# Output weights of three heads gathered onto chosen partitions in a cached attention block

## The chip, the cores and the metric

The kernel runs on one core of one Trainium2 chip. The metric is the device time of one execution in microseconds: 1310.93 us before the change, the median of 3 runs (1310.82 to 1311.02). All data is float32. The core's engines are TensorE (PE, matmuls), VectorE (DVE), ScalarE (ACT), GpSimd (POOL) and SyncE (SP, which issues nearly all transfers here), and it has 16 DMA engines that move data between HBM and the on-chip memory of 128 partitions.

## The reference

One token for each of two batch rows goes through a layer norm, then through attention over a cache of 32,768 keys and values, and through a gated projection:

```python
B, Sq, D = 2, 1, 512
Hq, Hkv, Sk, Dh = 32, 8, 32768, 128
xn = _layernorm(x)
q = (xn @ wq).reshape(B, Sq, Hq, Dh).transpose(0, 2, 1, 3)
scores = einsum("bhqd,bhkd->bhqk", q, k) * Dh ** -0.5      # 4 query heads share one key head
o = einsum("bhqk,bhkd->bhqd", softmax(scores), v)
s = o.transpose(0, 2, 1, 3).reshape(B, Sq, Hq * Dh) @ wo   # wo: 4096 x 512
h = relu(xn @ w1 + b1) ** 2                                # w1: 512 x 1792
g = silu(h @ w2 + b2)
out = x + s * g
```

The keys and the values are 268 MB each. `wo`, the output weights, is 8.4 MB: 32 heads of 128 rows of 512 numbers.

## The kernel before

The work goes in 16 steps `s`, one for each pair of key head and batch row (`hkv, b = divmod(s, B)`). For a step the keys come as two transfers of 8 MB (`load_k`, 64 KB for each of the 128 partitions, into three half slots `kslots`) and the values as two of 8 MB (`load_v`, into the one buffer `vbuf`). The main loop runs over 64 quarters `n` of keys: VectorE transposes the keys (L278), TensorE multiplies them with the queries (L283). After four quarters `softmax(s)` and `probs(s)` make the probabilities, and `values(m)` multiplies a values chunk with them (L358), two chunks behind. The queries stand in one of two buffers `qz`, which GpSimd fills for each step (`set_q`, L261).

All transfers of weights and cache stand in one list, `loads`, in the order in which SP issues them. An entry goes out when the event it names has passed in the program; the buffer's last reader is waited for on the chip. The last entries are the values of the last step and the output weights, which take the place of the keys.

The output projection is spread over 128 partitions. For eight heads at a time `load_wo(i)` gives each partition eight consecutive rows of `wo` (`"(p j) e -> p j e"`), and the attention output is laid out to match (`spread`, into `oW`). Head 0 stands apart: the rows of `wo` for the heads 1 to 31 go through `load_wo`, in pieces of 8, 8, 8 and then 4, 2 and 1 heads (`PIECES`, L138 and L142), while the 128 rows of head 0 come in the middle of the run. Ahead of the values chunks 8, 14, 20 and 26 (`FEW`) `load_few` issues two small transfers of 8 rows of 4 KB (two rows of `wo` together), onto the partitions 0 to 7 and 32 to 39 of the tile `few` (L148). `values` multiplies them (the matmuls of `project`, L403, into `few_ps`), multiplies by the gate and adds to the result `xe` (L347, L348). The selection of head 0's outputs for these partitions is `oF`, made in the branch `hkv == 0` of `values` (L384).

At the end the 24 + 7 heads of the wide loads are multiplied into `a_ps` (L403), multiplied by the gate (L468), added (L469) and stored (L471).

Of the kernel before, what the change touches and what calls it, by code (L numbers as in the profile page):

```python
# [8 lines left out]

F32 = mybir.dt.float32  # L10
AF = mybir.ActivationFunctionType
ALU = mybir.AluOpType
AX = mybir.AxisListType

P = 128
# [17 lines left out]

PIECES = ((0, 4), (4, 2), (6, 1))
FEW = (8, 14, 20, 26)
LAST = ((0, 64), (64, 128))

# [2 lines left out]
def gqa_decode_kernel(ctx: ExitStack, tc: tile.TileContext, x, kc, vc, wq, wo, w1, b1, w2, b2, out):  # L42
    nc = tc.nc
    B, _, D = x.shape
    _, HKV, SK, DH = kc.shape
    HQ = wq.shape[1] // DH
# [8 lines left out]
    WG = 8  # L55
    NWG = HQ // WG
# [6 lines left out]
    const = ctx.enter_context(tc.tile_pool(name="const", bufs=1))  # L63
    ktpool = ctx.enter_context(tc.tile_pool(name="ktpool", bufs=8))
    work = ctx.enter_context(tc.tile_pool(name="work", bufs=2))
# [66 lines left out]
    def load_wo(i):  # L132
        if i % 2 == 0:
            wide[i // 2] = kslots[:, 2 - i].rearrange("p (i j e) -> p i j e", i=2, j=WG)
        t = wide[i // 2][:, i % 2]
        base = (i * WG + 1) * P
        if i < NWG - 1:
            nc.sync.dma_start(t, wo[base:base + WG * P, :].rearrange("(p j) e -> p j e", p=P))  # L138
        else:
            for h0, nh in PIECES:  # L140
                lo = base + h0 * P
                nc.sync.dma_start(t[:, h0:h0 + nh, :], wo[lo:lo + nh * P, :].rearrange("(p j) e -> p j e", p=P))  # L142
        return t

    def load_few(i):
        for q in range(2):
            lo = 64 * q
            nc.sync.dma_start(few[32 * q:32 * q + 8].rearrange("p j e -> p (j e)"),  # L148
                              wo[lo:lo + 64, :].rearrange("(n y w j) e -> w y n (j e)", y=2, w=4, j=2)[i])

    wide = {}
    NK, NV = NS * NT, NS * NCH
    kslots = const.tile([P, 3, HALF], F32, name="kslots")
    few = const.tile([40, 2, D], F32, name="few")
    nc.gpsimd.memset(few, 0.0)
    vbuf = const.tile([P, 2 * HALF], F32, name="vbuf")
    loads = [(None, load_wq, 0), (None, load_half, 0), (None, load_half, 1), (("q", 0), load_w1, 0),
# [26 lines left out]
    ident = const.tile([P, P], F32, name="ident")  # L184
# [12 lines left out]
    selj = const.tile([P, WG], F32, name="selj")  # L197
    nc.vector.tensor_reduce(selj, ident.rearrange("p (e j) -> p j e", j=WG), axis=AX.X, op=ALU.add)
    sele = const.tile([P, P // WG], F32, name="sele")
    nc.vector.tensor_reduce(sele, ident.rearrange("p (e j) -> p e j", j=WG), axis=AX.X, op=ALU.add)  # L200
    sels = {}
    for nh in (4, 2):
        sels[nh] = const.tile([P, P // nh + nh], F32, name=f"sel_{nh}")
        nc.vector.tensor_reduce(sels[nh][:, 0:P // nh], ident.rearrange("p (e j) -> p e j", j=nh), axis=AX.X, op=ALU.add)
        nc.vector.tensor_reduce(sels[nh][:, P // nh:], ident.rearrange("p (e j) -> p j e", j=nh), axis=AX.X, op=ALU.add)
    oT = const.tile([P, HQ, B], F32, name="oT")
    oW = const.tile([P, NWG, WG, 16], F32, name="oW")
    nc.gpsimd.memset(oW, 0.0)
    oF = const.tile([40, WG, 32], F32, name="oF")
    nc.gpsimd.memset(oF, 0.0)  # L210
    sc = [pone.tile([P, 512], F32, tag=f"sc{i}", name=f"sc{i}") for i in range(NT)]
    o_ps = [pone.tile([P, 512], F32, tag=f"o{i}", name=f"o_ps{i}") for i in range(2)]
# [17 lines left out]
    t_ps = misc("xnT_ps")  # L230
# [107 lines left out]
    def values(n):  # L338
        s, k = divmod(n, NCH)
        vt = take(load_v, n)  # L340
        if n in FEW:
            i = FEW.index(n)
            take(load_few, i)
            t_ps = misc(f"few_ps{i}")
            project(t_ps, oF[:, 2 * i:2 * i + 2], few, 0, 2, start=True, stop=True)
            m = work.tile([P, DE], F32, tag="e", bufs=1, name=f"few{i}")
            nc.vector.tensor_mul(m, gate, t_ps[:, :DE])  # L347
            nc.vector.tensor_add(xe, m, xe)  # L348
        o = o_ps[s % 2]
# [12 lines left out]
        if k == NCH - 1:  # L362
            hkv, b = divmod(s, B)
            o_sb = work.tile([P, 512], F32, tag="o_sb", bufs=1, name=f"o_sb{s}")
            nc.scalar.copy(o_sb, o)  # L365
            t_ps = misc(f"oT_ps{s}")
            r4 = rs.pop(s)
            for i in range(4):
                nc.tensor.matmul(t_ps[:, :REP], o_sb[:, i * DH:(i + 1) * DH], r4[:, i, :], start=(i == 0), stop=(i == 3))  # L369
            nc.vector.tensor_copy(oT[:, hkv * REP:(hkv + 1) * REP, b], t_ps[:, :REP])  # L370
            i = hkv // 2
            t_ps = misc(f"oW_ps{s}")

            def spread(h0, nh, se, sj, x0):
                m = work.tile([P, P], F32, tag="om", bufs=1, name=f"om{s}_{h0}")
                nc.vector.tensor_mul(m.rearrange("p (h e) -> p h e", h=nh),
                                     oT[:, h0:h0 + nh, b:b + 1].to_broadcast([P, nh, P // nh]),
                                     se[:, None, :].to_broadcast([P, nh, P // nh]))
                nc.tensor.matmul(t_ps[:, x0:x0 + nh], m, sj, start=True, stop=True)

            if hkv == 0:
                m = work.tile([P, P], F32, tag="om", bufs=1, name=f"om{s}")
                for q in range(2):
                    nc.vector.tensor_mul(m[:, 32 * q:32 * q + 8].rearrange("p (y n) -> p y n", y=2),  # L384
                                         oT[:, 0:1, b:b + 1].to_broadcast([P, 2, 4]),
                                         sele[:, 8 * q:8 * q + 8].rearrange("p (n y) -> p y n", y=2))
                    nc.tensor.matmul(t_ps[32 * q:32 * q + 8, :WG], m[:, 32 * q:32 * q + 8], selj, start=True, stop=True)
                    nc.scalar.copy(oF[32 * q:32 * q + 8, :, b], t_ps[32 * q:32 * q + 8, :WG])
            elif hkv == HKV - 1:
                for h0, nh in PIECES[:-1]:  # L390
                    spread(i * WG + 1 + h0, nh, sels[nh][:, 0:P // nh], sels[nh][:, P // nh:], h0)
                h0 = PIECES[-1][0]
                nc.scalar.copy(oW[:, i, 0:h0, b], t_ps[:, 0:h0])
                nc.vector.tensor_copy(oW[:, i, h0, b:b + 1], oT[:, HQ - 1, b:b + 1])
            elif hkv % 2 == 0:
                spread((i - 1) * WG + 1, WG, sele, selj, 0)
                nc.scalar.copy(oW[:, i - 1, :, b], t_ps[:, :WG])


    def project(a_ps, ow, wt, j0, j1, start=False, stop=False):  # L400
        for j in range(j0, j1):
            for g in range(NG):
                nc.tensor.matmul(a_ps[32 * g:32 * g + ow.shape[-1], :DE], ow[:, j, :], wt[:, j, g * DE:(g + 1) * DE],  # L403
                                 start=start and j == j0, stop=stop and j == j1 - 1)
# [20 lines left out]
    def mlp_down():  # L425
        wt = take(load_w2, 0)
        y_ps = misc("y_ps")
        for g in range(NG):
            nc.tensor.matmul(y_ps[32 * g:32 * g + 32, :DE], ones[0:1, 0:32], b2t[:, g * DE:(g + 1) * DE],
                             start=True, stop=False)  # L430
        for j in range(FJ):
            for g in range(NG):
                nc.tensor.matmul(y_ps[32 * g:32 * g + 32, :DE], hT[:, j, :], wt[:, j, g * DE:(g + 1) * DE],
                                 start=False, stop=(j == FJ - 1))
        give("w", 1)
        e = work.tile([P, DE], F32, tag="e", bufs=1, name="e")
        nc.scalar.activation(e, y_ps[:, :DE], AF.Sigmoid)
        nc.vector.tensor_mul(gate, e, y_ps[:, :DE])


    for n in range(NK):
        s, i = divmod(n, NT)
        if i == 0:
            set_q(s)
        scores(n)
        if n == 1:
            mlp_up()
        if n == 3:
            mlp_down()
        if i == 3:  # L450
            softmax(s)
        if n >= 5 and n % 2 == 1:
            values((n - 5) // 2)
        if i == 3:
            probs(s)
# [7 lines left out]
    for i in range(NWG - 1):  # L463
        project(a_ps, oW[:, i], wot[i], 0, WG, start=(i == 0))
    for h0, nh in PIECES:
        project(a_ps, oW[:, NWG - 1], wot[NWG - 1], h0, h0 + nh, stop=(h0 + nh == WG - 1))
    asb = work.tile([P, DE], F32, tag="e", bufs=1, name="a_sb")
    nc.vector.tensor_mul(asb, gate, a_ps[:, :DE])  # L468
    nc.vector.tensor_add(xe, asb, xe)  # L469
# [25 lines left out]
```

## Time and profile before

| | |
|---|---|
| median of 3 runs | 1310.93 us (1310.82 to 1311.02) |
| the profiled execution's own time | 1310.78 us |
| its span, first to last instruction | 1309.0 us |
| busy: PE, DVE, ACT, POOL | 893.6 (68%), 653.2 (50%), 88.7 (7%), 15.8 (1%) us |
| bytes moved by DMA | 561.75 MB, mean 429 GB/s |
| last transfer of output weights in the chain | issued at 1272.84 us, 31.40 us |
| mean granted TensorE clock | 0.843 |

A line of the page or of an answer names the source line (L283 is line 283 of the kernel), the engine, the operation, the tile written and the tiles read, the shape, how often, the busy time and the mean duration, then the idle time of the engine just before, with what ended it. `SPq` is SP's queue of issues. The DMA rows give packets, MB and the share of the span of 16 engines that their packets took. The windows view cuts the span into stretches and gives each engine's busy time and the share of the 16 DMA engines at work. The chain is followed back from the last instruction to whatever released each step.

### The profile page before, as it was taken

Reading aid. Unit: us, or ns where it says so; the run is one execution under the profiler, and the core shown is the slowest. Engines: PE = TensorE matmul, PEld = TensorE weight load, DVE = VectorE, ACT = ScalarE, POOL = GpSimd, SP = SyncE. Lnnn points to the kernel's source line nnn. Section 1 sums busy time; section 2 is a strip of 40 time slices with the busy share of each in tenths; the row PEclk is TensorE's granted clock in tenths of the full one; section 3 lists DMA queues with packets and bytes.
Section 4 is the critical chain, followed back from the end, with each engine's and each line's share of the span. In section 5 each row is a group of like instructions: output and inputs, shape, how many; then the busy total and the mean of one; then the engine's idle time right before and its main releaser. Section 6 shows DMA issues by size and latency. Waiting matters only on the chain.

```text
span 1309.0 us, 11687 instructions
## 1 busy us (share of the span) xinstructions
PE 893.6 (68%) x4994; PEld 252.4 (19%) x4994; DVE 653.2 (50%) x762; ACT 88.7 (7%) x241; POOL 15.8 (1%) x78
## 2 busy tenths in 40 slices
PE   3867675758757567765757767566875657777575
PEld 1222121212212121111212212121221112212122
DVE  2855654435555344664435565444655534566410
ACT  0010010101001010000101001010100101001010
POOL 0000000000000000000000000000000000000000
PEclk9988887789877789887889887788987878887788
DMA  9999999999999999999999999999999999999997
GB/s 404 432 442 431 431 435 429 439 427 439 429 433 433 435 427 439 425 443 421 442 425 439 432 429 437 425 439 427 437 431 433 435 431 434 429 431 437 427 427 325
DMA packets 11121, 561.75 MB, mean 429 GB/s; under 512 B 1255, under 2 KB 1275, under 8 KB 1598
## 3 DMA queue, kind: packets, MB, share of 16 engines
q1 hardware_dynamic: 11032, 561.00, 99.3%
q8 instruction: 39, 0.64, 0.2%
q14 instruction: 12, 0.10, 0.0%
q10 hardware_dynamic: 38, 0.02, 0.0%
HBM read 561.01 MB, written 0.00 MB: 429 GB/s over the span
## 4 chain that ended last, share of the span: by engine, by line
DMA 74%; DVE 19%; issue 5%; PE 2%; DVEq 0%; ACTq 0%; SPq 0%
DMA kslots<-in_A_k_cache 68%; DVE kt L278 18%; DMA kslots<-in_A_wo 2%; DMA kslots<-in_A_v_cache 2%; DMA first_p<-in_A_x 1%; PE sc L241 1%; PE o_ps L358 0%; PE h_ps L415 0%; DVE qr L248 0%; PE qT_ps L252 0%; DVEq L278 0%; PE sc L283 0%; PE xnT_ps L232 0%; PE sc L403 0%; DVE h L422 0%
## 5 line engine op out<-in xcount | busy, mean ns | idle before, releaser
L283 PE MATMUL sc<-kt,qz 128*32 128x512 f32 x2048 | 577.4, 669 | 321.9 <-DVE kt L278 300.0
L278 DVE STREAM_TRANSPOSE kt<-kslots 128x1024 f32<-128x1024 f32 x512 | 580.7, 1204 | 341.0 <-DMA kslots<-in_A_k_cache 340.9
L283 PEld LDWEIGHTS sc<-kt,qz 128*32 128x32 f32 x2048 | 111.6, 115 | 775.3 <-DVE kt L278 580.9
L358 PE MATMUL o_ps<-vbuf,pT 128*16 128x512 f32 x1984 | 229.5, 599 | 9.2 <-DMA vbuf<-in_A_v_cache 9.2
L358 PEld LDWEIGHTS o_ps<-vbuf,pT 128*16 128x16 f32 x1984 | 75.2, 97 | 140.4 <-issue 121.7
L305 ACT ACTIVATE p<-sc,nm 128x512 f32<-128x512 f32 x32 | 23.2, 741 | 988.4 <-DVE nm L301 988.4
L370 DVE COPY oT<-oT_ps 128x4 f32<-128x4 f32 x16 | 2.6, 162 | 123.3 <-PE oT_ps L369 123.3
L288 DVE TENSOR_REDUCE rm<-sc 128x1 f32<-128x512 f32 x32 | 22.1, 691 | 63.9 <-PE sc L283 63.9
L324 ACT COPY pT<-pT_ps 64x256 f32<-64x256 f32 x128 | 46.8, 366 | 18.8 <-PE pT_ps L320 17.3
L330 DVE RECIPROCAL r<-l_ps 128x4 f32<-128x4 f32 x16 | 2.9, 182 | 47.3 <-PE l_ps L328 47.3
L261 POOL COPY qz<-qT 32x16 f32<-32x16 f32 x64 | 12.7, 198 | 1076.6 <-PE sc L283 1041.9
L369 PE MATMUL oT_ps<-rs,o_sb 128*128 128x4 f32 x128 | 16.9, 255 | 11.7 <-ACT o_sb L365 11.7
L320 PE MATMUL pT_ps<-ident,p 128*128 128x128 f32 x128 | 21.8, 317 | 3.2 <-ACT p L305 2.9
L369 PEld LDWEIGHTS oT_ps<-rs,o_sb 128*128 128x128 f32 x128 | 15.5, 191 | 25.8 <-ACT o_sb L365 25.8
L328 PE MATMUL l_ps<-lh,ones 128*128 128x4 f32 x32 | 8.4, 333 | 16.1 <-ACT pT L324 16.1
L320 PEld LDWEIGHTS pT_ps<-ident,p 128*128 128x128 f32 x128 | 17.4, 169 | 4.0 <-ACT p L305 3.1
L365 ACT COPY o_sb<-o_ps 128x512 f32<-128x512 f32 x16 | 9.4, 585 | 101.9 <-PE o_ps L358 101.9
L308 DVE TENSOR_REDUCE l<-l 128x1 f32<-128x2 f32 x16 | 2.5, 155 | 26.8 <-ACT p L305 26.8
L232 PE MATMUL xnT_ps<-ident,xn 128*128 128x128 f32 x4 | 1.1, 431 | 21.1 <-DVE xn L228 21.1
L294 PE MATMUL mx_ps<-ident,rm 128*128 128x128 f32 x16 | 5.0, 316 | 15.0 <-DVE rm L292 15.0
L358 PE MATMUL o_ps<-kslots,pT 128*16 128x512 f32 x64 | 8.9, 718 | 4.6 <-DMA kslots<-in_A_v_cache 4.6
L328 PEld LDWEIGHTS l_ps<-lh,ones 128*128 128x128 f32 x32 | 7.0, 273 | 20.7 <-ACT pT L324 20.7
(85 smaller groups left out, 131.1 us busy)
## 6 DMA issues: line engine op xcount, KB each, us to landing
kslots<-in_A_k_cache SPq DMA_DIRECT2D x4, 4096.0 KB
vbuf<-in_A_v_cache SPq DMA_DIRECT2D x2, 4096.0 KB
vbuf<-in_B_w SPq DMA_DIRECT2D x2, 3584.0 KB
kslots<-in_A_wo SPq DMA_DIRECT2D x3, 2048.0 KB
kslots<-in_A_wo SPq DMA_DIRECT2D x1, 1024.0 KB
kslots<-in_A_wo SPq DMA_DIRECT2D x1, 512.0 KB
kslots<-in_A_k_cache SPq DMA_DIRECT2D x30
vbuf<-in_A_v_cache SPq DMA_DIRECT2D x30
```

Source lines behind the costliest of these rows:

```text
L241: nc.tensor.matmul(sc[f][32 * g:32 * g + 32, :], xnT[:, d, 0:32], wqt[:, d, cc * 512:(cc + 1) * 512], start=(d == 0), stop=(d == ND - 1))
L261: nc.gpsimd.tensor_copy(qz[s % 2][32 * a:32 * a + 32, 16:].rearrange("p (e y) -> p e y", e=4)[:, :, a * REP:(a + 1) * REP], qT[32 * a:32 * ...
L278: nc.vector.transpose(r.rearrange("p e o w -> p o e w"), kt[:, g * NO:(g + 1) * NO, e0 * 32:(e0 + 2) * 32].rearrange("p o (e w) -> p o e w ...
L283: nc.tensor.matmul(bank[32 * g:32 * g + 32, :], qz[s % 2][:, lo + 32 * (e0 + e):lo + 32 * (e0 + e) + 32], kts[g][:, e].rearrange("p o w -> ...
L288: nc.vector.tensor_reduce(rm[s][:, u:u + 1], bank, axis=AX.X, op=ALU.max)
L305: nc.scalar.activation(p[:, :, :, u], sc[2 * (s % 2) + u].rearrange("p (o w) -> p o w", w=32), AF.Exp, bias=nm, scale=SCALE, accum_out=l2[ ...
L320: nc.tensor.transpose(t_ps[:, j * P:(j + 1) * P], p[:, o:o + 2].rearrange("p o w u -> p (o w u)"), ident)
L324: nc.scalar.copy(sb[64 * a:64 * a + 64].rearrange("p k g c (i j o) h -> p i o j (g c) k h", i=2, o=2)[:, i, o], v[:, :, :, :, a])
L328: nc.tensor.matmul(t_ps[:, :REP], ones, lh, start=True, stop=True)
L358: nc.tensor.matmul(o[32 * y:32 * y + 16, :], pT[s][:, k, g, c, 4 * i:4 * i + 4, :].rearrange("p o h -> p (o h)"), vt[:, lo:lo + 4, :].rear ...
L365: nc.scalar.copy(o_sb, o)
L369: nc.tensor.matmul(t_ps[:, :REP], o_sb[:, i * DH:(i + 1) * DH], r4[:, i, :], start=(i == 0), stop=(i == 3))
```

## The change

The heads 0, 1 and 2 (`NF = 3`) leave the wide loads, which now hold the heads 3 to 31 in pieces of 8, 8, 8, 4 and 1 heads. Their 384 rows of `wo` are taken as 192 rows of 4 KB by six indirect DMAs that GpSimd issues, in four portions at the places where the small transfers stood (`load_few`). The tile `few` has 128 partitions now; 48 of them are used, each with one 4 KB row a portion, thus 8 rows of `wo` in all. They are picked by pairs of numbers from 0 to 15 (`PAIRS`): number `e` stands for the partitions `first_part(e)` to `first_part(e) + 3` and the same plus 32. Head 0 goes to the numbers 0 and 1, head 1 to 4 and 5, head 2 to 14 and 15. Partitions that a gather leaves out have an index beyond the table (`SKIP`), and the DMA passes over them. The first portion is two gathers (numbers 0, 1, 4, 5, and 14, 15), the second too (0, 4, 14, and 1, 5, 15), the others one each.

The indices are computed on the chip (`set_fidx`, called at `n == 6`): GpSimd writes a 128x128 tile with every partition's index in its column, VectorE converts it, multiplies it by the identity and sums each row. In the order in which the engines get their instructions, the index work stands in the pause after the first step's scores, ahead of and between the steps of the first softmax; the first two gathers stand on GpSimd's queue there, the others later. The selection in the branch `hkv == 0` is 12 small multiplies for a batch row, one 128-row matmul and one copy, where it was two of each.

```diff
-PIECES = ((0, 4), (4, 2), (6, 1))
+PAIRS = ((0, 1), (4, 5), (14, 15))
+NF = len(PAIRS)
+GATHERS = ((0, (0, 1, 4, 5)), (0, (14, 15)), (1, (0, 4, 14)), (1, (1, 5, 15)), (2, (0, 1, 4, 5, 14, 15)),
+           (3, (0, 1, 4, 5, 14, 15)))
+SKIP = 100000
+PIECES = ((0, 4), (4, 1))
...
     def load_few(i):
-        for q in range(2):
-            lo = 64 * q
-            nc.sync.dma_start(few[32 * q:32 * q + 8].rearrange("p j e -> p (j e)"),
-                              wo[lo:lo + 64, :].rearrange("(n y w j) e -> w y n (j e)", y=2, w=4, j=2)[i])
+        for c, (piece, _) in enumerate(GATHERS):
+            if piece == i:
+                nc.gpsimd.indirect_dma_start(few.rearrange("p j e -> p (j e)"), None, wo.rearrange("(n j) e -> n (j e)", j=2),
+                                             bass.IndirectOffsetOnAxis(ap=fidx[:, c:c + 1], axis=0),
+                                             bounds_check=HQ * P // 2 - 1, oob_is_err=False)
...
             if hkv == 0:
-                m = work.tile([P, P], F32, tag="om", bufs=1, name=f"om{s}")
-                for q in range(2):
-                    nc.vector.tensor_mul(m[:, 32 * q:32 * q + 8].rearrange("p (y n) -> p y n", y=2),
-                                         oT[:, 0:1, b:b + 1].to_broadcast([P, 2, 4]),
-                                         sele[:, 8 * q:8 * q + 8].rearrange("p (n y) -> p y n", y=2))
-                    nc.tensor.matmul(t_ps[32 * q:32 * q + 8, :WG], m[:, 32 * q:32 * q + 8], selj, start=True, stop=True)
-                    nc.scalar.copy(oF[32 * q:32 * q + 8, :, b], t_ps[32 * q:32 * q + 8, :WG])
+                for h, pair in enumerate(PAIRS):
+                    for x, e in enumerate(pair):
+                        lo = first_part(e)
+                        for q in range(2):
+                            nc.vector.tensor_mul(mF[:, lo + 32 * q:lo + 32 * q + 4], oT[:, h, b:b + 1].to_broadcast([P, 4]),
+                                                 sele[:, 8 * q + 4 * x:8 * q + 4 * x + 4])
+                nc.tensor.matmul(t_ps[:, :WG], mF, selj, start=True, stop=True)
+                nc.scalar.copy(oF[:, :, b], t_ps[:, :WG])
...
+    def first_part(e):
+        return 64 * (e // 8) + 4 * (e % 8)
+
+    def set_fidx():
+        for c, (i, queues) in enumerate(GATHERS):
+            wi = work.tile([P, P], I32, tag="tmp", name=f"wi{c}")
+            nc.gpsimd.iota(wi, pattern=[[0, P]], base=SKIP, channel_multiplier=0)
+            for h, pair in enumerate(PAIRS):
+                for x, e in enumerate(pair):
+                    if e in queues:
+                        for q in range(2):
+                            lo = first_part(e) + 32 * q
+                            nc.gpsimd.iota(wi[:, lo:lo + 4], pattern=[[4, 4]], base=h * P // 2 + 4 * (8 * q + 4 * x) + i,
+                                           channel_multiplier=0)
+            wf = work.tile([P, P], F32, tag="om", bufs=1, name=f"wf{c}")
+            nc.vector.tensor_copy(wf, wi)
+            nc.vector.tensor_mul(wf, wf, ident)
+            ws = work.tile([P, 1], F32, tag="rm", name=f"ws{c}")
+            nc.vector.tensor_reduce(ws, wf, axis=AX.X, op=ALU.add)
+            nc.vector.tensor_copy(fidx[:, c:c + 1], ws)
...
+        if n == 6:
+            set_fidx()
```

More of the change, by code (lines that the diff above doesn't have):

```diff
@@ L10 @@
 F32 = mybir.dt.float32
+I32 = mybir.dt.int32
 AF = mybir.ActivationFunctionType
@@ L135, in load_wo @@
         t = wide[i // 2][:, i % 2]
-        base = (i * WG + 1) * P
+        base = (i * WG + NF) * P
         if i < NWG - 1:
@@ L153, in gqa_decode_kernel @@
     kslots = const.tile([P, 3, HALF], F32, name="kslots")
-    few = const.tile([40, 2, D], F32, name="few")
+    few = const.tile([P, 2, D], F32, name="few")
+    fidx = const.tile([P, len(GATHERS)], I32, name="fidx")
     nc.gpsimd.memset(few, 0.0)
@@ L201, in gqa_decode_kernel @@
     sels = {}
-    for nh in (4, 2):
+    for nh in (4,):
         sels[nh] = const.tile([P, P // nh + nh], F32, name=f"sel_{nh}")
@@ L208, in gqa_decode_kernel @@
     nc.gpsimd.memset(oW, 0.0)
-    oF = const.tile([40, WG, 32], F32, name="oF")
+    oF = const.tile([P, WG, 32], F32, name="oF")
+    mF = const.tile([P, P], F32, name="mF")
+    nc.gpsimd.memset(mF, 0.0)
     nc.gpsimd.memset(oF, 0.0)
@@ L381, in values @@
             if hkv == 0:
-                m = work.tile([P, P], F32, tag="om", bufs=1, name=f"om{s}")
-                for q in range(2):
-                    nc.vector.tensor_mul(m[:, 32 * q:32 * q + 8].rearrange("p (y n) -> p y n", y=2),
-                                         oT[:, 0:1, b:b + 1].to_broadcast([P, 2, 4]),
-                                         sele[:, 8 * q:8 * q + 8].rearrange("p (n y) -> p y n", y=2))
-                    nc.tensor.matmul(t_ps[32 * q:32 * q + 8, :WG], m[:, 32 * q:32 * q + 8], selj, start=True, stop=True)
-                    nc.scalar.copy(oF[32 * q:32 * q + 8, :, b], t_ps[32 * q:32 * q + 8, :WG])
+                for h, pair in enumerate(PAIRS):
[6 more added lines that the diff above has]
+                nc.scalar.copy(oF[:, :, b], t_ps[:, :WG])
             elif hkv == HKV - 1:
                 for h0, nh in PIECES[:-1]:
-                    spread(i * WG + 1 + h0, nh, sels[nh][:, 0:P // nh], sels[nh][:, P // nh:], h0)
+                    spread(i * WG + NF + h0, nh, sels[nh][:, 0:P // nh], sels[nh][:, P // nh:], h0)
                 h0 = PIECES[-1][0]
@@ L395, in values @@
             elif hkv % 2 == 0:
-                spread((i - 1) * WG + 1, WG, sele, selj, 0)
+                spread((i - 1) * WG + NF, WG, sele, selj, 0)
                 nc.scalar.copy(oW[:, i - 1, :, b], t_ps[:, :WG])
+    def first_part(e):
[17 more added lines that the diff above has]
+            nc.vector.tensor_copy(fidx[:, c:c + 1], ws)
     def project(a_ps, ow, wt, j0, j1, start=False, stop=False):
@@ L465, in gqa_decode_kernel @@
     for h0, nh in PIECES:
-        project(a_ps, oW[:, NWG - 1], wot[NWG - 1], h0, h0 + nh, stop=(h0 + nh == WG - 1))
+        project(a_ps, oW[:, NWG - 1], wot[NWG - 1], h0, h0 + nh, stop=(h0 + nh == WG - NF))
     asb = work.tile([P, DE], F32, tag="e", bufs=1, name="a_sb")
```

## The prediction

> **What bounds the kernel now.** I read the page first, then the windows view by stretches, then the chain that ended last. The page's DMA picture and queues:
>
> ```profile
> span 1309.0 us, 11687 instructions
> ...
> q1 hardware_dynamic: 11032, 561.00, 99.3%
> q8 instruction: 39, 0.64, 0.2%
> ...
> L278 DVE STREAM_TRANSPOSE kt<-kslots 128x1024 f32<-128x1024 f32 x512 | 580.7, 1204 | 341.0 <-DMA kslots<-in_A_k_cache 340.9
> ```
>
> SP's queue (q1) keeps the 16 DMA engines at work for 99.3% of the span, and the busiest line of VectorE waits 340.9 us for keys. One engine's rate follows: 561.00 MB / (0.993 x 16 x 1309.0 us) = 26.97 KB per us. The windows view says where the sixteen are not all at work:
>
> ```profile
> core 0: us, PE busy (x) PEld busy (x) DVE busy (x) ACT busy (x) POOL busy (x), PEclk, DMA share, GB/s
> 100.00:300.00 200.00, 138.91 (x705) 38.17 (x706) 104.66 (x116) 10.72 (x30) 1.59 (x8) 0.82 1.00 432
> 900.00:1200.00 300.00, 204.30 (x1071) 57.15 (x1061) 151.23 (x173) 20.49 (x54) 2.38 (x12) 0.82 1.00 432
> 1297.00:1298.00 1.00, 1.00 (x16) 0.98 (x20) 0.07 (x1) 0.00 (x0) 0.00 (x0) 1.00 0.76 320
> 1298.00:1299.00 1.00, 1.00 (x28) 0.77 (x24) 0.45 (x3) 0.00 (x0) 0.00 (x0) 1.00 0.69 295
> 1299.00:1300.00 1.00, 1.00 (x22) 0.76 (x24) 0.29 (x1) 0.13 (x1) 0.00 (x0) 1.00 0.64 270
> 1300.00:1301.00 1.00, 1.00 (x38) 0.72 (x30) 0.00 (x0) 0.04 (x1) 0.00 (x0) 1.00 0.68 283
> 1301.00:1302.00 1.00, 1.00 (x47) 1.00 (x40) 0.00 (x0) 0.00 (x0) 0.00 (x0) 1.00 0.72 299
> 1302.00:1303.00 1.00, 0.54 (x20) 0.26 (x12) 0.00 (x0) 0.00 (x0) 0.00 (x0) 1.00 0.59 227
> 1303.00:1304.00 1.00, 0.86 (x32) 0.81 (x32) 0.00 (x0) 0.00 (x0) 0.00 (x0) 1.00 0.45 178
> 1304.00:1304.50 0.50, 0.42 (x16) 0.22 (x12) 0.00 (x0) 0.00 (x0) 0.00 (x0) 1.00 0.20 74
> ```
>
> The next to last column is the share of the 16 engines that is at work. It is 1.00 through the middle, so no engine waits for an issue there: each works through its own list without a break, and the end is set by the engine with the longest list. From 1298 to 1302 the share averages 0.68, so 5.1 of 16 engines have already finished; the others stop between 1302 and 1304.5. Idle room in the tail is 0.24 + 0.31 + 0.36 + 0.32 + 0.28 + 0.41 + 0.55 + 0.5 x 0.80 = 2.87 us, times 16 = 46 engine-us.
>
> Why are the lists unequal, when each 128-partition transfer gives all engines the same? Two loads are uneven. The 39 instruction packets are 0.2% of 16 x 1309.0 us, 42 engine-us (31 to 52 by the rounding), 1.07 us for each 16 KB, where q1's rate would take 0.61. And the eight small transfers of head 0:
>
> ```profile
> few<-in_A_wo SPq DMA_DIRECT2D x8, 32.0 KB
> ```
>
> are 64 rows of 4 KB, 0.152 us each at 26.97 KB per us, 9.7 engine-us. Followed packet after packet in the trace's records (no view prints them, and they carry no engine number), the instruction packets return to the same streams throughout, the small rows sit on two others, and streams with neither finish first. The chain shows the small rows holding up the keys:
>
> ```profile
> 263.28 29.52 DMA kslots<-in_A_k_cache
> 302.05 30.94 DMA kslots<-in_A_k_cache
> ...
> 1272.84 31.40 DMA kslots<-in_A_wo
> 1304.28 0.63 PE sc L403 x16
> 1304.92 0.46 PE sc L403 x8
> ```
>
> The transfer issued at 302.05 has the first two small ones just ahead of it and takes 1.42 us longer than its neighbour; eight rows of 0.152 us are 1.22. After the last weights have landed there is only TensorE's remainder, two VectorE operations and the store.
>
> **The change part by part.** *Removed from every engine:* heads 1 and 2 leave the wide loads, 2 x 262,144 B / 16 = 32 KB, 1.21 us per engine. All of it is on the path, since the longest list decides: -1.2 us.
>
> *Added to chosen engines:* three heads are 192 rows of 4 KB. In the code's numbering six DMA engines get 32 rows each, 4.9 us. Destinations 0 and 1 are the partitions 0-7 and 32-39 that take head 0 today, also 32 rows on each of two engines, so nothing is added there. Four others get 4.9 us more. If these are engines that stop by about 1297.5, they will stop at 1297.5 - 1.2 + 4.9 = 1301.2, before the long lists at 1304.4 - 1.2 = 1303.2: cost nothing, cover 2.0 us.
>
> *Price of a row from GpSimd's queue.* The trace has no DMA of that queue. The nearest row is q1's own 4 KB rows, 0.152 us, and I take it, since size, source and engines are the same. The dear end is the instruction queue's rate, 1.07 / 4 = 0.27 us: 32 rows would be 8.6 us, the four would end at 1304.9, and the two that bear 4.9 us today would move by -1.2 + 3.7 = +2.5 us. A row cheaper than 0.152 would only widen the cover, so nothing is gained below -1.2.
>
> Which engine a row lands on no row tells. In the Trainium skill, DMA: Bandwidth & Descriptors, section "The descriptor swizzle", a 128-partition transfer puts partitions p and p + 32 of one group of four on the same engine, which is what the code's formula inverts; the page states it for plain transfers, and no run here shows it for a gather.
>
> *SP:* eight issues leave its queue, and with them the delay seen at 302.05; both only shift work among engines that are never idle, so nothing beyond the terms above.
>
> *Building the indices* (the helper `set_fidx`). The first gather and part of the index work stand in the pause after the first score group:
>
> ```profile
> 83.35 0.15 DVE L292 TENSOR_REDUCE rm<-rm 128x1 f32<-128x2 f32 x1
> 85.94 0.29 DVE L296 TENSOR_REDUCE mh<-mx_ps 128x4 f32<-128x128 f32 x1 [2.43 <-PE mx_ps L294]
> ...
> 91.98 0.18 DVE L332 TENSOR_TENSOR rs<-selg,r 128x16 f32<-128x16 f32 x1
> 99.26 1.25 DVE L278 STREAM_TRANSPOSE kt<-kslots 128x1024 f32<-128x1024 f32 x1 [7.11 <-DMA kslots<-in_A_k_cache]
> ...
> L261 POOL COPY qz<-qT 32x16 f32<-32x16 f32 x64 | 12.7, 198 | 1076.6 <-PE sc L283 1041.9 <-ACT qT L255 31.8
> L376 DVE TENSOR_TENSOR om<-oT,sele 128x128 f32<-128x128 f32 x6 | 1.8, 292 | 0.2
> L384 DVE TENSOR_TENSOR om<-oT,sele 128x8 f32<-128x8 f32 x4 | 0.5, 162 | 0.1
> L148 SPq DMA_DIRECT2D few<-in_A_wo x8: 607/634/797, 281.5 to 983.4; - x8
> ...
> L155 POOL MEMSET few<- 40x1024 f32 x1 | 0.9, 948 | 0.0
> POOL qz L261 <- PE sc L283: 1041.9, 14, 78.0
> ```
>
> The first view is VectorE's timeline around the first softmax, the others are groups of instructions, SP's small issues and GpSimd's waits (us in total, times, longest). VectorE gains 24 operations here, six times a copy, a multiply and a reduction of 128x128 (0.29 each) and a 128x1 copy (0.16): 1.03 x 6 = 6.2 us. GpSimd writes six index tiles with 6 fills and 48 small writes; at 0.198 each that is 10.7 us. Three of the tiles come before the pause; in it stand the first gather and 33 writes, 6.5 us, and VectorE's last index steps wait for them with the softmax behind (6.2 us from 85.94 to 92.16). From 83.5: 1.2 for the first index, 0.6 for the gather's issue (taken from SP's 634 ns), 6.5, 1.0 and 6.2 end at 99.0, against 99.26 when the next keys land. So the cover is used up; behind it is another. The key transfer issued at 263.28 took 29.52 us, of which its 8.39 MB (128 x 64 KB) at 432 GB/s are 19.4, so it stood 10.1 us behind the values. A key issue that is late by less than that leaves no engine idle. Taken: 0. The end without the gather issue at all is 0 too; a long one is a rival below.
>
> *The selection for head 0 to 2:* 12 small multiplies instead of 2 for each batch, 10 x 0.162 = 1.6 us of VectorE twice, beside waits that average 340.9 / 30 = 11 us. One 128-row matmul replaces two small ones, beside a TensorE that waits as well. Nothing.
>
> *GpSimd's queue:* from the third gather on, each waits until the rows before it have been used, and the next query copies (L261) stand behind it. They sit 1041.9 us in 14 waits for the score group before, the longest 78.0, so this costs nothing; it would if the copies came later than the scores' own start.
>
> *The last loads:* pieces of 4 and 1 heads instead of 4, 2 and 1. The last piece stays 256 KB. The 4-head piece now ends about 0.7 us ahead of it, and its 32 matmul records, at 0.63 / 16 each, are 1.26 us, against 0.63 + 0.46 after the landing today: from -0.1 to +0.4 us, taken as 0.
>
> The sum: 1309.0 - 1.2 = 1307.8 of span. The profiled execution took 1310.78, that is 1.78 outside the span, so 1309.6; it lies 0.15 below the median of the runs, 1310.93, so 1309.7.
>
> **The rivals.** *B, the rows are dealt out over all sixteen.* If the generator deals the listed rows round the engines and not by partition, each gets 12 rows, 1.8 us. The longest lists move by -1.2 + 1.8 = +0.6: 1311.5. For it: the skipped rows, 80 or more of 128 in each gather, leave the generator free. Against: head 0's rows stay on two streams today.
>
> *C, at least one of the four new destinations already has a long list; this ends slower.* 1304.4 - 1.2 + 4.9 = 1308.1, +3.7 us: 1314.6; with the dear row, -1.2 + 8.6 = +7.4: 1318.3. It decides as soon as such an engine stops today later than 1304.4 - 4.9 = 1299.5, where 0.64 of the engines are still at work. For it: only 5 of 16 have stopped by then, and no view names them. The same page of the Trainium skill, section "Why a DMA increments its semaphore by 16 and not by 1", says that some transfers from GpSimd give each engine a block of consecutive partitions; by that the 48 partitions form six blocks of eight, on engines 0, 2, 4, 6, 11 and 15, and the time would be C's if one of 2, 4, 6, 11 and 15 is long. No run here shows which. Against: exactly these early engines are as many as four places need. In between, A': an engine that stops in the middle, about 1302 (0.72 still at work from 1301), ends at 1305.7, +1.3: 1312.2.
>
> *D, the first gather's issue is long.* VectorE's softmax and then the transposes are queued behind it; beyond about 10.1 us the engines run dry once, us for us. At 15 us it costs 5: 1314.7. Against: GpSimd's longest instruction in the trace, a fill of 40x1024, takes 0.948.
>
> *E, the rows are better placed than I think:* with all room in the tail filled the bound is -2.87 us, 1308.1. That needs every engine to stop together, which rows in portions of 4.9 us don't give.
>
> *That the change doesn't do what it says:* the gathers sit on GpSimd's queue as told, though the first two are free to start in the pause at 84 us, not in the middle. Since the engines are never idle either way, this alters no number.
>
> **How the numbers follow.** A (1309.7) 0.44, A' (1312.2) 0.13, B (1311.5) 0.10, C 0.20 with the cheap row and 0.03 with the dear one, D 0.04, E 0.06. A's own range, with the dear row on the two old destinations, is 1309.7 to 1313.4 (1310.93 + 2.5). Against 0.2% (2.6 us, about what a measurement of this kernel can tell from no change) A, A' and B count as the same, 0.67; C and D as slower, 0.27; E as faster, 0.06. The range leaves out the dear C, the worst of D and E: 1309.0 to 1315.0, with 0.4 to 0.7 us around the outer cases for the coarse shares.
>
> **What would show it.** Right: a DMA share of 1.00 in the middle, in the tail's windows more engines at work from 1297 to 1301 than today's 0.64 to 0.76, the last weights landing 1.2 us earlier, and key transfers in the chain without the extra 1.4 us just behind the small rows. C shows as a tail share well under 0.45 for some 4 us, B as an unchanged tail that ends later, D as a hole in the DMA share near 100 us and a late first key issue. The prediction is wrong if a gather makes the engines idle in the middle, or if its rows take more than 0.27 us.

## The result, and the profile after

The changed kernel takes 1315.47 us, median of 8 runs (six at 1315.17 to 1315.59, two at 1313.97 and 1314.01), against 1310.99 us of the kernel before (8 runs): a ratio of 1.0032, 95% interval 1.0021 to 1.0043. It is 4.5 us slower, where 1309.7 was forecast, with a range of 1309.0 to 1315.0. The profiled execution took 1315.38 us, its span is 1313.5.

The page of the changed kernel, the span and the DMA queues (packets, MB, share of the span of 16 engines), to be laid beside the queues shown before:

```profile
span 1313.5 us, 11739 instructions
...
q1 hardware_dynamic: 10808, 560.21, 98.8%
q8 instruction: 39, 0.64, 0.2%
q0 software_dynamic: 864, 0.79, 0.2%
```

One queue is new, q0, that of GpSimd's gathers. It moves 0.79 MB (192 rows of 4 KB), but in 864 packets: the other 672 are 4-byte packets, 576 for the skipped indices and 96 completions (6 gathers, one on each of 16 engines). In the trace's packet records, which no view prints, a row takes 0.159 us and a 4-byte packet 9 ns: 192 x 0.159 + 672 x 0.009 = 36.6 engine-us, which agrees with the 0.2% (of 16 x 1313.5 us: 32 to 53).

The windows view of the changed kernel, one stretch of the middle and then the tail, in the columns shown before (the next to last is the share of the 16 DMA engines at work):

```profile
core 0: us, PE busy (x) PEld busy (x) DVE busy (x) ACT busy (x) POOL busy (x), PEclk, DMA share, GB/s
900.00:1200.00 300.00, 201.60 (x1077) 54.52 (x1076) 148.16 (x171) 20.53 (x54) 2.39 (x12) 0.83 1.00 433
...
1298.00:1299.00 1.00, 1.00 (x8) 0.19 (x4) 0.00 (x0) 0.00 (x0) 0.00 (x0) 0.50 0.93 389
1299.00:1300.00 1.00, 1.00 (x12) 0.22 (x8) 0.00 (x0) 0.00 (x0) 0.00 (x0) 0.55 0.98 410
1301.00:1302.00 1.00, 0.86 (x16) 0.42 (x10) 0.00 (x0) 0.44 (x1) 0.00 (x0) 1.00 0.54 223
1303.00:1304.00 1.00, 1.00 (x26) 0.77 (x25) 0.52 (x3) 0.00 (x0) 0.00 (x0) 1.00 0.24 94
1305.00:1306.00 1.00, 0.48 (x23) 0.20 (x16) 0.00 (x0) 0.00 (x0) 0.00 (x0) 1.00 0.09 25
1306.00:1307.00 1.00, 1.00 (x44) 1.00 (x40) 0.00 (x0) 0.00 (x0) 0.00 (x0) 1.00 0.12 49
1307.00:1308.00 1.00, 0.80 (x32) 0.52 (x20) 0.00 (x0) 0.00 (x0) 0.00 (x0) 1.00 0.09 37
```

The middle is full as before (1.00), so nothing was lost there. The tail has another shape. Before, 0.64 to 0.76 of the engines worked until 1302 and all stopped by 1304.5. Now 0.93 and 0.98 are at work to 1300, nearly all have stopped by 1304, and from 1305 to 1308 the share is 0.09 to 0.12, which is 1.4 to 1.9 of 16: two engines work alone for some 4 us. This is what the prediction named as the sign of rival C, "a tail share well under 0.45 for some 4 us".

The end of the chain that ended last, of the changed kernel:

```profile
1277.12 31.17 DMA kslots<-in_A_wo
1308.42 1.32 PE sc L436 x40
```

The weights of this row land at 1277.12 + 31.17 = 1308.29, against 1272.84 + 31.40 = 1304.24 before: 4.05 us later. They are the last piece but one, of four heads now and of two before; by the packet records the last head's piece ends 0.65 us behind it in both kernels, so also 4.05 us later. Behind the landing TensorE has 40 matmuls, eight for each of five heads, in 1.32 us, where it had 16 in 0.63 and 8 in 0.46.

### The profile page after: what moved, and what is told of

The parts are those of the page before. It is cut to its first block, busy times and chain, and to the rows that moved or that the text cites. A ratio compares the mean times of both kernels' runs of the same rounds, so it can differ in the third digit from the quotient of the medians.

```text
span 1313.5 us, 11739 instructions
## 1 busy us (share of the span) xinstructions
PE 892.0 (68%) x4970; PEld 247.1 (19%) x4970; DVE 658.5 (50%) x802; ACT 88.7 (7%) x239; POOL 27.4 (2%) x139
## 4 chain that ended last, share of the span: by engine, by line
DMA 74%; DVE 18%; issue 5%; PE 2%; DVEq 0%; POOL 0%; SPq 0%; POOLq 0%
DMA kslots<-in_A_k_cache 68%; DVE kt L288 18%; DMA kslots<-in_A_wo 2%; DMA kslots<-in_A_v_cache 2%; DMA vbuf<-in_A_wq 2%; PE sc L251 1%; PE o_ps L368 0%; PE h_ps L448 0%; DVE qr L258 0%; PE qT_ps L262 0%; DVEq L288 0%; PE sc L293 0%; PE sc L436 0%; DVE h L455 0%; DVE hr L452 0%
## 5 line engine op out<-in xcount | busy, mean ns | idle before, releaser
L368 PEld LDWEIGHTS o_ps<-vbuf,pT 128*16 128x16 f32 x1984 | 70.1, 97 | 148.5 <-issue 126.6
```

## The experiments

After the result two theories stood. *Theory 1*: the loss is rival C, some of the four new destinations lie on DMA engines whose lists were long already. *Theory 2*: the gathers cost time wherever their rows land. Every kernel below was compared with the kernel before on the same chip; that one took 1310.96, 1311.03, 1311.02 and 1311.01 us in the four groups.

**1 and 2: other pairs.** In the first, head 1 goes to the numbers 2 and 3, head 2 to 4 and 5; in the second, to 2 and 3, and 14 and 15.

```diff
-PAIRS = ((0, 1), (4, 5), (14, 15))
+PAIRS = ((0, 1), (2, 3), (4, 5))      # 1
+PAIRS = ((0, 1), (2, 3), (14, 15))    # 2
```

> As the changed kernel, but the third head's rows go to the numbers 2 and 3 in place of 14 and 15 (pairs 0 1, 2 3, 4 5). Theory 1: the rows cost what a 4 KB row takes (0.159 us), and the loss comes from two of the four new destinations, which had long lists already; if those are 14 and 15, this kernel loses the late pair and gains the 1.2 us of the two heads: 1309.8 us. Theory 1 with 4 and 5 as the long ones: 1315.5, as the changed kernel. Theory 2: gathers from GpSimd's queue cost time wherever the rows land: 1315.5.

> As the changed kernel, but the second head's rows go to the numbers 2 and 3 in place of 4 and 5 (pairs 0 1, 2 3, 14 15). Theory 1 with 14 and 15 as the long lists: 1315.5 us; with 4 and 5 as the long lists: 1309.8. Theory 1 with one long list in each pair: 1315.5 here and with 2 3 4 5. Theory 2 (a gather costs time wherever its rows land): 1315.5.

Measured: 1315.22 us (1.0033, interval 1.0020 to 1.0045) and 1315.53 (1.0033, 1.0021 to 1.0046). Both have two late engines in the tail (shares of 0.10 to 0.16 from 1305 to 1307, where one engine is 0.06), as the changed kernel has. With one pair exchanged each time and still two late engines, each of the pairs (2, 3), (4, 5) and (14, 15) holds one long list. By themselves these two don't part the theories, since a cost of the gathers would be the same in all.

**3: one head gathered.** Head 0 alone, on the numbers 0 and 1 where it was before, but by four gathers in place of eight transfers of SP's queue; the wide loads and the last pieces are those of the kernel before.

```diff
-PAIRS = ((0, 1), (4, 5), (14, 15))
+PAIRS = ((0, 1),)
-PIECES = ((0, 4), (4, 1))
+PIECES = ((0, 4), (4, 2), (6, 1))
```

> Only head 0 is gathered, in four gathers of 16 rows to the numbers 0 and 1, where the kernel before sends the same rows from SP's queue; the wide loads are those of the kernel before. Theory 1: within 0.5 us of the kernel before, 1311.0, since the same two engines carry the same rows. Theory 2: the 5.7 us by which the changed kernel misses the sum, taken as a price of its six gathers, is 0.95 us for each of the four here: 1314.8.

Measured: 1311.29 us, 1.0002 (0.9993 to 1.0012). The gather as such, with its index building and its place on GpSimd's queue, costs 0.3 us by the medians, and the interval holds no change too. Theory 2 falls as an explanation of 4.5 us. The 0.3 is of the size of the small packets: 512 of 9 ns on 16 engines are 0.29.

**4: no small rows.** The kernel before with all 32 heads in the wide loads.

```diff
-PIECES = ((0, 4), (4, 2), (6, 1))
+PIECES = ((0, 4), (4, 2), (6, 1), (7, 1))
...
-        if m in FEW:
-            loads.append((None, load_few, FEW.index(m)))
```

> The kernel before without small rows: all 32 heads go through the wide loads (pieces 8, 8, 8 and 4, 2, 1, 1). Theory 1: every engine gets 16 KB more, 0.61 us, the two with the small rows get 5.1 us less; the engines with the instruction packets keep the end, so +0.6: 1311.6 us, and the share of engines at work in the tail falls, as seven instead of five finish early. Rival: the two engines with the small rows set the end before, then up to 4.3 us faster: 1306.7.

Measured: 1311.53 us, 1.0005 (0.9996 to 1.0014), 0.57 above the kernel before. One head is 262,144 B / 16 = 16 KB for each engine, 0.61 us at 26.97 KB per us. That fits the term by which the change was to gain, 0.61 us for each head off the wide loads, though the interval (0.5 us faster to 1.8 slower) is wide. The time did not fall when 5 us of rows left two streams, so these had ended ahead of the longest. Its tail in the windows view:

```profile
1299.00:1300.00 1.00, 1.00 (x26) 0.77 (x22) 0.36 (x2) 0.00 (x0) 0.00 (x0) 1.00 0.51 213
1301.00:1302.00 1.00, 1.00 (x45) 1.00 (x41) 0.00 (x0) 0.06 (x1) 0.00 (x0) 1.00 0.57 238
1302.00:1303.00 1.00, 1.00 (x47) 1.00 (x39) 0.00 (x0) 0.00 (x0) 0.00 (x0) 1.00 0.55 221
```

With the small rows gone, and by the packet records no uneven load left but the instruction packets, the share stands between 0.51 and 0.57 for some four microseconds: about seven of the 16 engines have stopped and nine are still at work.

The packet records of this run show where the nine lose the time. They carry no engine number, but the next packet of an engine starts within 4 ns of the end of the one before, so an engine's stream can be followed from packet to packet. From one key or values transfer to the next, a stream without an instruction packet keeps its distance from the first engine (median change 0.00 us of 861), and one with a 16 KB instruction packet falls back by 1.55 us (median of 31): the packet takes 1.07, and the 64 KB packet behind it 2.91 in place of 2.42. Shortly before the end nine streams stand 6.1 to 8.4 us behind the first, which is about four or five such packets, and the other seven at most 2.2.

**5 and 6: two numbers exchanged.** Two heads are gathered in seven gathers, head 0 on 0 and 1, head 1 on 2 and 4 in one kernel and on 3 and 5 in the other; nothing else differs between the two, and the last pieces are 4, 1 and 1 heads in both. Which numbers to try came from the packet records: of the streams with gathered rows some reach the same point of the keys 7 to 8 us behind the first engine, the others 3 to 5. The gathers of the second portion hold three of the six numbers each, so the count of late streams in each gather leaves two readings: 3, 5 and 14 are long, or 2, 4 and 15.

```diff
-PAIRS = ((0, 1), (2, 4))
+PAIRS = ((0, 1), (3, 5))
```

> Two heads gathered (head 0 to the numbers 0 and 1, head 1 to 2 and 4), the other thirty wide, the last pieces 4, 1 and 1 heads; each portion after the first in two gathers of two numbers, so that the trace tells which streams are late. Theory 1 (the loss comes from new destinations whose DMA engines also carry the instruction packets), in the reading that 3, 5 and 14 are such engines: no new destination is one, so one head off every list counts, -0.6 us: 1310.4 us. The other reading of the same traces, that 2, 4 and 15 are: 1304.4 - 0.6 + 32 x 0.159 = 1308.9, +4.5: 1315.5 us. Theory 3 (more than one gathered head costs something wherever it goes): above 1312, and the same as with the numbers 3 and 5.

> The same kernel with head 1 on the numbers 3 and 5 in place of 2 and 4; nothing else differs. Theory 1, 3 and 5 carry instruction packets: both get 5.1 us more at the end of a long list, 1315.5 us, with two late engines in the tail. The other reading (2, 4 and 15): 1310.4 us. Theory 3: the same time as with 2 and 4.

Measured: 1311.33 us with 2 and 4 (1.0002, 0.9993 to 1.0011) and 1315.99 with 3 and 5 (1.0037, 1.0023 to 1.0051). The two tails in the windows view, first with 2 and 4, then with 3 and 5:

```profile
1298.00:1299.00 1.00, 0.66 (x13) 0.36 (x5) 0.00 (x0) 0.58 (x1) 0.00 (x0) 1.00 0.83 352
1302.00:1303.00 1.00, 1.00 (x47) 1.00 (x41) 0.00 (x0) 0.00 (x0) 0.00 (x0) 1.00 0.53 215
1304.00:1305.00 1.00, 1.00 (x48) 1.00 (x40) 0.00 (x0) 0.00 (x0) 0.00 (x0) 1.00 0.10 39
1305.00:1306.00 1.00, 0.56 (x22) 0.28 (x11) 0.34 (x2) 0.00 (x0) 0.00 (x0) 1.00 0.00 0
```

```profile
1302.00:1303.00 1.00, 0.82 (x14) 0.30 (x6) 0.00 (x0) 0.47 (x1) 0.00 (x0) 1.00 0.69 277
1305.00:1306.00 1.00, 1.00 (x14) 0.76 (x14) 0.29 (x1) 0.00 (x0) 0.00 (x0) 1.00 0.12 49
1307.00:1308.00 1.00, 1.00 (x48) 1.00 (x40) 0.00 (x0) 0.00 (x0) 0.00 (x0) 1.00 0.11 43
1308.00:1309.00 1.00, 1.00 (x48) 1.00 (x40) 0.00 (x0) 0.00 (x0) 0.00 (x0) 1.00 0.21 64
```

The same rows, bytes, gathers and instructions, and 4.66 us between them. On 2 and 4 they fill room in the tail (0.83 at 1298, where the kernel before had 0.69) and no engine works past 1305; on 3 and 5 the share is 0.11 and more up to 1309. Rows therefore land by their number, and which numbers they are decides the loss; theory 3 of the expectations, that a second gathered head costs something wherever it goes, falls as well. The first kernel came out 0.9 above what was expected of it; half of that is found below. Some of the rest is on TensorE, whose work behind the last values ends this kernel: in the profile those values' matmuls took 6.53 us at a granted clock of 0.50, against 5.24 before, where the clock was 0.50 for only three of the microseconds, and the 134 matmuls from 1301.66 on run without a pause.

The Trainium skill, DMA: Bandwidth & Descriptors, section "The descriptor swizzle", states the formula that the code inverts, for plain transfers. The gathers here agree with it: in the packet records the 16 rows of a gather onto two numbers sit on two streams, eight on each. Blocks of eight consecutive partitions, which the prediction weighed beside rival C, would spread the rows of 2 and 4 over four streams, four on each.

**7 and 8: the other numbers.** Two heads on 6, 7, 8 and 9, and on 10, 11, 12 and 13, again in seven gathers, so that each number's stream can be told by the pairs it comes in.

```diff
-PAIRS = ((0, 1), (2, 4))
+PAIRS = ((6, 7), (8, 9))         # 7
+PAIRS = ((10, 11), (12, 13))     # 8
```

> The same kernel with head 0 on the numbers 6 and 7 and head 1 on 8 and 9. Theory 1 counts eight engines with instruction packets, three of them among 0 to 5, 14 and 15, so five among 6 to 13 and at least one in each four of these: 1315.5 us, with as many late engines in the tail as long lists among the four, and late streams in the gathers that tell which. Were none of 6 to 9 long: 1310 us, and the count of eight would be wrong.

> The same kernel with head 0 on the numbers 10 and 11 and head 1 on 12 and 13. Theory 1: at least one of them long, 1315.5 us; the late engines here and with 6 to 9 should be five together. Were none long: 1310 us.

Measured: 1315.78 us (1.0036, 1.0022 to 1.0050) and 1316.08 (1.0038, 1.0025 to 1.0052). In the first, the gather of 6 and 9 has both streams some 8.5 us behind the first engine, that of 7 and 8 both 3 to 4; in the second all four are 8.3 to 8.6 behind by the third portion. So 3, 5, 6 and 9 to 14 are long, nine of them and not eight, which agrees with the share of experiment 4, and 0, 1, 2, 4, 7, 8 and 15 are not. Experiment 9 will test 2, 4, 7 and 15 in one kernel; that 8 is short rests on its stream alone. The tail with 10 to 13:

```profile
1305.00:1306.00 1.00, 1.00 (x27) 0.78 (x28) 0.00 (x0) 0.17 (x1) 0.00 (x0) 1.00 0.22 90
1306.00:1307.00 1.00, 1.00 (x43) 1.00 (x44) 0.00 (x0) 0.00 (x0) 0.00 (x0) 1.00 0.23 98
```

Here 0.22 to 0.23, some four engines, are late, and yet the time is that of experiment 6 with two: the longest list counts, not how many there are.

**9, 10 and 11: the rows on short lists, and the price of a gather.** In 9 the changed kernel has 2 and 7 in place of 5 and 14; 10 has one gather a portion instead of six in all; 11 adds to it, in each portion, two gathers whose indices are all beyond the table. (The gathers of 9 keep their shape, with the new numbers; 11 has one more entry `(9, ())` at the end of `GATHERS`, whose indices are all `SKIP`.)

```diff
-PAIRS = ((0, 1), (4, 5), (14, 15))
+PAIRS = ((0, 1), (4, 2), (7, 15))                                     # 9, 10, 11
-GATHERS = ((0, (0, 1, 4, 5)), (0, (14, 15)), (1, (0, 4, 14)), ...
+GATHERS = ((0, (0, 1, 4, 2, 7, 15)), (1, (0, 1, 4, 2, 7, 15)), ...    # 10, 11
-        for c, (piece, _) in enumerate(GATHERS):
+        for c in [c for c, (piece, _) in enumerate(GATHERS) if piece == i] + 2 * [len(GATHERS) - 1]:   # 11
```

> The changed kernel with two of its six numbers replaced: 2 for 5 and 7 for 14; as many rows, gathers and pieces as before. Theory 1, by now: the engines of 3, 5, 6, 9 to 14 have long lists, those of 0, 1, 2, 4, 7, 8 and 15 have not. No row lies on a long list then, and the loss of 4.5 us is gone: the two heads that leave the wide loads count, -1.21 us, less what 672 small packets of the gathers (576 skipped rows and 96 completions, 9 ns each) take from each of 16 engines, 0.38 us: 1311.0 - 1.21 + 0.38 = 1310.2 us. A rival, that three gathered heads cost something wherever they go, or that 7 is long: 1314 us or more.

> The same with one gather in each portion (four instead of six) on the numbers 0, 1, 2, 4, 7 and 15: 384 small packets, 0.22 us for each engine: 1311.0 - 1.21 + 0.22 = 1310.0 us, the version that should beat both kernels, if only by less than a measurement can tell. If a gather costs more than its packets (0.13 us each, as the kernel with two heads on 0, 1, 2 and 4 would have it: 0.94 us above 1310.4 with 7 gathers): 1310.3.

> The kernel with one gather a portion and, behind each, two more gathers whose 128 indices are all beyond the table: no data, 8 x 144 small packets more. By the packets' 9 ns: +0.65 us against the one without them, 1310.65. By 0.13 us for each gather: +1.0, 1311.3. If skipped rows cost nothing: no difference.

Measured: 9 takes 1310.73 us (0.9998, 0.9989 to 1.0007), 10 takes 1310.73 (the same interval), 11 takes 1311.29 (1.0003, 0.9994 to 1.0012). Two numbers out of six take back 4.7 of the changed kernel's 1315.47. The windows view of 9:

```profile
1299.00:1300.00 1.00, 1.00 (x29) 0.77 (x24) 0.25 (x2) 0.17 (x1) 0.00 (x0) 1.00 0.95 401
1303.00:1304.00 1.00, 0.46 (x20) 0.20 (x12) 0.00 (x0) 0.00 (x0) 0.00 (x0) 1.00 0.31 117
1304.00:1305.00 1.00, 1.00 (x40) 0.90 (x36) 0.00 (x0) 0.00 (x0) 0.00 (x0) 1.00 0.00 0
```

This is the tail that the prediction described: 0.95 at work where it was 0.64, and nothing after 1304. Eight empty gathers cost 0.56 us by the medians, 0.07 each; by 144 packets of 9 ns on 16 engines it would be 0.08. The DMA share stays 1.00 from 100 to 1200 us in that kernel, so no engine ran dry for them. So skipped rows aren't free, they are what a gather costs here. (That 11 meets the 1311.3 of the dearer reading is luck: experiment 10, from which it was reckoned, came out 0.4 us above that reading's own 1310.3.) Between 9 and 10 the packets would make 0.16 us, which their medians don't show.

What keeps 10 from the forecast 1309.7 shows at the end of its chain:

```profile
1272.36 31.09 DMA kslots<-in_A_wo
1303.59 1.32 PE sc L435 x40
```

The weights land at 1303.45, 0.79 us ahead of before (-1.21 for two heads and +0.22 for 384 small packets make -0.99; 0.2 stays unexplained). But then 40 matmuls stand behind the landing, and the span is only 0.3 shorter. Nor would an earlier landing have brought much in this execution, since TensorE had waited only 0.17 us for it.

**12: the last pieces 2, 2 and 1 heads.** The kernel of 10 with its last transfers cut finer.

```diff
-PIECES = ((0, 4), (4, 1))
+PIECES = ((0, 2), (2, 2), (4, 1))
```

> The kernel with one gather a portion on the numbers 0, 1, 2, 4, 7 and 15 (1310.73 us), its last transfers cut into 2, 2 and 1 heads in place of 4 and 1. If TensorE's remainder after the last landing is what kept that kernel from showing the whole of its 0.8 us earlier landing (40 matmuls in 1.32 us, where the kernel before had 16 in 0.63 and 8 in 0.46): 0.25 us less, 1310.45. If the landing of the last 256 KB alone sets the end: no difference, 1310.7.

Measured: 1310.38 us (1309.83 to 1310.69), 0.9995 (0.9985 to 1.0004), 0.35 less than 10. The end of its chain:

```profile
1273.67 30.25 DMA kslots<-in_A_wo
1303.96 1.08 PE sc L435 x24
```

24 matmuls and 1.08 us are left where 40 and 1.32 were. This execution (1310.59 us) isn't the median one and its weights landed at 1303.92, later than in 10. TensorE works without a pause from 1300.59 to 1305.00 here, so its own work now ends together with the landing. The 0.35 stands in the medians alone, which agree with a shorter remainder but don't show it, and the runs of 10 and 12 overlap a little at 1310.6. This is the fastest version here, 0.63 us under the kernel before, though the interval still reaches 1.0004.

## Why the prediction was wrong

**The step that failed is "Four others get 4.9 us more ... cost nothing, cover 2.0 us".** It rested on "if these are engines that stop by about 1297.5". Two of the four aren't: 5 and 14 carry long lists, 4 and 15 don't. Rival C, which said just this, is what happened. The forecast saw that only five engines stop early and that no view names them, and then gave the good case 0.44 because five "are as many as four places need". That was no evidence. Of the 14 engines besides head 0's two, five stop early; four places taken blindly all fall on early ones once in 14 x 13 x 12 x 11 / (5 x 4 x 3 x 2) = 200 times. Without a name for the engines the rival ought to have been the forecast, at 1314.6.

**The size of C** was 0.9 us short, and the measured time lies 0.47 beyond the range. C's sum, -1.2 + 4.9 = +3.7, against the landing's +4.05 and the median's +4.48. A row takes 0.159 us and not 0.152, so 32 are 5.09 (+0.2). The 672 small packets of the gathers, 0.38 us for each engine, were not in the sum; experiment 11 is evidence that they count (0.56 us for 1152 of them, where 0.65 was reckoned). With both, -1.21 + 5.09 + 0.38 = +4.26 for the landing. And the last pieces, "taken as 0" between -0.1 and +0.4, cost: the changed kernel ends 1308.42 + 1.32 = 1309.74 on TensorE, 4.36 after 1305.38 of before, so 0.3 more than the landing. Experiment 12 took 0.35 back by the medians. The same two terms are 0.57 of the 0.9 us by which the good case, once it was made (experiment 10), stayed short of the gain of 1.21, and the small packets are half of the 0.9 by which experiment 5 stood above its 1310.4: with 7 gathers it has 880 of them, 0.50 us.

**What the prediction misread in the profile before.** It took the key transfer of 30.94 us issued at 302.05 as held up by head 0's small rows, and its end as a sign of success. The kernel without any small rows (experiment 4) has the same transfer:

```profile
263.36 29.52 DMA kslots<-in_A_k_cache
...
302.13 30.98 DMA kslots<-in_A_k_cache
```

In both kernels the packet records have a 16 KB instruction packet 5 us into this transfer, on one of the streams that were last (from 2.1 us behind the first engine to 3.7), which accounts for the delay of some 1.4. The changed kernel has 29.57 us at 303.47, so the sign appeared although the prediction was wrong. The instruction packets were also counted at 1.07 us each; what they cost their stream is 1.55. Neither changes the forecast's sum, but both hid what made the long lists long.

**What was right.** The gain of 0.61 us for each head (experiment 4: 0.57). That the longest list decides, and rows land by number and not dealt round (B). That the middle stays full. The dear row of 0.27 us didn't come.

**The indices were hidden, by a wider margin than worked out.** The pause after the first scores, in the timeline of the changed kernel:

```profile
85.09 1.23 POOL L154 DMA_INDIRECT few<-in_A_wo,fidx  x1 [1.22 <-DVE ws L429]
...
95.72 0.17 DVE L342 TENSOR_TENSOR rs<-selg,r 128x16 f32<-128x16 f32 x1
99.21 11.38 DVE L288 STREAM_TRANSPOSE kt<-kslots 128x1024 f32<-128x1024 f32 x10 [3.31 <-DMA kslots<-in_A_k_cache]
```

And its groups of instructions on GpSimd (busy time in all, mean ns of one, idle time before):

```profile
L154 POOL DMA_INDIRECT few<-in_A_wo,fidx x6 | 6.3, 1050 | 89.0 <-issue 28.3 <-DVE rm L298 24.7 <-DMA few<-in_A_wo,fidx 21.5
L423 POOL IOTA wi<- 128x4 int32 x48 | 3.9, 131 | 0.1
```

The softmax's last step ends at 95.89 (before 92.16, worked out 99.0), and the next keys' transposes start at 99.21, against 99.26 before, so the keys were not held up. A small index write takes 131 ns, not 198; a gather's issue 1.05 us, 1.23 for the first, about twice the 0.6 taken, and far from the 10 us that rival D needed.

**What stays open.** That the long lists are long because of the instruction packets is read from the packet records: the step of 1.55 us at each packet, and where the packets lie. On the stretches of streams that can be followed around the gathered rows, those of 10 to 13 have 9 packets of q8 beside 1022 of 64 KB, and those of 0, 1, 2, 4, 7 and 15 have 0 and 1 beside some 1540 (experiments 9 and 10), where an even spread would give 7. No kernel here moved those packets, so no experiment shows their part. What the experiments show is which numbers are late. Why the packets lie on these nine engines isn't known. Nor is it settled why two of the eight runs took 1314.0.

## What to carry to other kernels

Where all DMA engines are busy to the end, a few extra rows cost nothing or cost all of their time, and only the engine on which they land decides which; find out which engines end early before choosing, by putting rows on a few and reading the tail's share, and until then reckon the chance by counting the engines, not by hope. The packets of a gather's skipped indices count as work on every engine (0.07 us for each empty gather here), so few gathers, each with many rows, should be cheaper than many; between six and four no difference could be seen. What a smaller transfer total brings at the last landing can be lost to the matmuls behind it, so the last pieces should be looked at again when the sizes change. And the cause that a prediction gives for a slow transfer is cheap to test: take the supposed cause out and see whether the transfer is still slow.

## What the runs showed of the hardware

- An index beyond the table still costs: a gather of 128 indices leaves 128 packets and 16 completions whatever it moves (864 for six, 576 for four, 1728 for twelve); eight that moved nothing cost 0.56 us, 0.07 each. That every engine completes, also without data, is what the Trainium skill, DMA: Bandwidth & Descriptors, section "Why a DMA increments its semaphore by 16 and not by 1", states for GpSimd's transfers; the count of packets agrees.
- A gather in the middle of full queues takes long to land, since its rows wait between the keys' packets of 64 KB, and the second gather of the first portion waited for it. The gathers among the changed kernel's DMA issues (the last column is the median time from issue to landing):

```profile
few<-in_A_wo,fidx POOLq DMA_INDIRECT x6, 25.0
```

  And GpSimd's waits (in total, times, longest):

```profile
POOL few L154 <- DMA few<-in_A_wo,fidx: 21.5, 1, 21.5
```

  Eight rows of 0.159 us are 1.3 us of an engine's work, and land after 25.0. No cost of it can be seen: with one gather a portion none waits for another, and the time is that of six gathers (experiments 10 and 9).
- A 16 KB instruction packet amid 64 KB packets cost its stream 1.55 us, not only its own 1.07: the next 64 KB packet took 2.91 us in place of 2.42.
- With equal data for all, seven of the 16 engines ended some 4 us and more ahead of the other nine, and the numbers that were read off on one chip held on the next one (experiments 5 to 8 and 9 to 12).
